# DeltaNet with an FNet block on one core: another way to the inverses of the first three rounds, a rebuilt first chain and earlier loads

## The chip, the cores and the metric

The kernel runs on one core of a Trainium2 chip. The metric is the device time in microseconds (us). Engines are named as in the profile: PE (TensorE, matmuls), PEld (its weight loads), DVE (VectorE), ACT (ScalarE), POOL (GpSimd), SP (SyncE, which here only issues DMAs).

## The reference

Four sequences of 768 tokens, 8 heads of 48, go through a delta rule; the output, 384 wide, goes through an FNet block. All in float32 (the weights come as float64).

```python
for t in range(S):
    kt, vt, bt = (k_n[:, :, t], v[:, :, t], beta[:, :, t, None])
    y[:, :, t] = np.einsum('bhd,bhde->bhe', q[:, :, t], state)
    v_old = np.einsum('bhde,bhd->bhe', state, kt)
    state = state + bt[:, :, :, None] * np.einsum('bhd,bhe->bhde', kt, vt - v_old)
...
X = np.fft.fft(x, axis=1)
X = np.fft.fft(X, axis=2)
mixed = np.real(X).astype(np.float32)
u = x + mixed
...
ch = np.maximum(un @ w_ch1, 0.0) @ w_ch2
return (u + ch).astype(np.float32)
```

`k_n` is k divided by its norm, `un` is u with mean and variance taken out.

## The kernel before

A tile `g` is 128 tokens of all 8 heads of one batch; a batch has 6 tiles (`NL`), there are 24. A chunk (`c`) is 64 tokens (`C`); inside a chunk the recursion is solved by the inverse of a unit lower triangular 64 x 64 matrix for every head. Four tiles (`RL`) make a round `r`; its matrices are inverted together.

- `pre_a(g)` turns the keys of a tile (KT) and forms their Gram products: the diagonal 32 x 32 blocks go to `G`, the blocks beside them to `GX` (X).
- `invert(r)`: 1024 blocks of 32 x 32 lie as 128 partitions x 8 x 4 after a 32 x 32 transpose on DVE (line 312). Norms follow (319 to 343, the root on ACT), then forward substitution: 31 steps, each a product `tmp` (353) and a sum into `M` (357). Two transposes (360, 361) bring the result back, into `A` and `G`.
- `pre_m(g)` joins the two 32-blocks of a chunk: two batches of 16 products of 32 x 32 (G,GX and A,XM), whose results ACT copies to XM and MT (419, 430). V is scaled by the norms on POOL (402). For batch 0 it goes on to WT and U0, products of MT with K and V (445, 447).
- `pre_q(g)` turns queries (QT) and forms the masked products LQ with the keys; for batch 0 all six are made ahead, the mask on POOL (391).
- `step(g, c)` carries the state S over a chunk: a product with S, a subtraction on DVE (498 for batch 0, 476 later), a product with K, an addition on DVE (517). This is the chain from chunk to chunk. `outputs(g)` writes the tile of x (541, 551).
- `fourier(b)`: folds of x (568 to 579, the first two on POOL), sums over the sequence with the tables evt and odt (590), over the width with dtab (611), then norms (617 to 629). `mlp(b)` makes ph and hT (660, 662), po (668) and the output.
- `weights()` turns the float64 words into float32: 12 pieces, each a row of five steps over ACT, DVE and POOL (235 to 250), six of `w1` and six of `w2`; a piece waits for the buffers of the one before it.

Generators yield after a step of work, and the code at the end interleaves them. Batch 0 stands in a block where the order on PE, DVE, ACT and POOL is the order of the program (785): keys of rounds 0 and 1, `invert(0)` with `invert(1)` woven in, then a loop over 12 chunks (835) in which the chain, the next tile's `pre_m`, the rest of `invert(1)`, the conversion of `w1` and two of the three folds take turns; then keys of round 2 with the sums of `fourier(0)`. After it (865) the order is fixed on PE alone: `mlp(b)` is spread over the `period(g)` of the next batch (six slots each), and `invert(r + 1)` runs on DVE beside them; the first period with tiles of a new round drains it (763). At a batch's end `weave` (868) spreads 12 pieces of the mlp over `fourier(b)`.

Keys for `pre_a` are loaded into three rotating buffers `Cs`, queries into two (`Qs`), both by SP; a load waits until its buffer was turned.

Of the kernel before, what the change touches and what calls it, by code (L numbers as in the profile page):

```python
# [17 lines left out]
C = 64  # L18
L = 128
W = 32  # L20
RL = 4
RING = 7


def _consts(S, DM):
# [6 lines left out]
    pack = np.concatenate([ident, su, blk], axis=1)  # L32
# [27 lines left out]
def kernel(  # L60
# [79 lines left out]

    def load_c(g, engine=None):
        if g < NLT:
            (engine or nc.sync).dma_start(out=Cs[g % 3][:, :, 0:D], in_=rows(k, g))

    def load_q(g):
        if g < NLT:
            nc.sync.dma_start(out=Qs[g % 2][:, :, 0:D], in_=rows(q, g))
# [12 lines left out]
    def load_beta(r):  # L160
# [5 lines left out]
        while i < RL:  # L166
            b, n = divmod(RL * r + i, NL)
            m = min(RL - i, NL - n)
            for q4 in range(4):
                hh, blk = divmod(q4, 2)  # L170
                p0 = q4 * W + i * 8
                src = beta[b, 4 * hh:4 * hh + 4, n * L:(n + m) * L].rearrange(
                    "j (c b t) -> b c j t", b=2, t=W)[blk]
                nc.sync.dma_start(out=t[p0:p0 + 8 * m], in_=src)
            i += m
        betas[r] = t

    pack = const.tile([128, 128 + C + 2], F32, name="pack")
    nc.scalar.dma_start(out=pack, in_=cn["pack"].ap())
    load_c(0)  # L180
    load_c(1, nc.scalar)
    load_c(2)
    load_beta(0)
    ident = pack[:, 0:128]
    m_su = pack[:, 128:128 + C]
    m_blk = pack[:, 128 + C:128 + C + 2]

# [4 lines left out]
    w2 = const.tile([128, KF, DM], F32, name="w2")  # L192

    low_e = const.tile([128, 1], F32, name="low_e")
    nc.gpsimd.memset(low_e, -896.0)
    half_n = const.tile([128, GT], F32, name="half_n")
# [78 lines left out]
    def pre_a(g):  # L275

        K = Cs[g % 3]
        r, li = divmod(g, RL)
        KT = KTs[g] = wk.tile([128, 2, 2, 128], F32, tag="KT", bufs=RING, name="KT")
        turn(KT, K)  # L280
        load_c(g + 3)
# [3 lines left out]
        X = GXs[g] = wk.tile([128, 8, W], F32, tag="GX", bufs=8, name="GX")  # L285
        pg = ps_pair()
        for i in range(4):
            c, jj = divmod(i, 2)
            for q4 in range(4):
                for jp in range(2):  # L290
# [3 lines left out]
                    if blk:  # L294
# [4 lines left out]
        nc.scalar.activation(Gs[r][:, 8 * li:8 * li + 8].rearrange("p (i a) s -> p a i s", a=2),  # L299
                             src[:, :, :, 0:W], ACT.Copy)  # L300
        nc.scalar.activation(X.rearrange("p (i a) s -> p a i s", a=2), src[:, :, :, W:C],
                             ACT.Copy)
        yield

    def invert(r):
# [3 lines left out]
        M = wk.tile([128, W, W], F32, tag="x" if r == 1 else "M", bufs=2 if r == 1 else 1,  # L309
                    name="M")  # L310
# [53 lines left out]

    LQs = {}

    def pre_q(g, QT=None, LQ=None):

        Q, KT = Qs[g % 2], KTs[g]
        early = QT is not None  # L370
# [5 lines left out]
        load_q(g + 2)  # L376
# [12 lines left out]
        if early:  # L389
            nc.scalar.activation(dst, src, ACT.Copy)  # L390
            nc.gpsimd.tensor_tensor(dst, dst, mask, op=ALU.mult)
        else:
            nc.vector.tensor_tensor(dst, src, mask, op=ALU.mult)
        yield

    def pre_m(g):

        r, li = divmod(g, RL)
        K, V, X = Ks[g % 3], Vs.pop(g), GXs.pop(g)
# [16 lines left out]
        XM = wk.tile([128, 8, W], F32, tag="XM", name="XM")  # L416
# [11 lines left out]
        for hh in range(2):  # L428
            rw = slice(64 * hh, 64 * hh + W)
            nc.scalar.activation(MT[rw, :, 1, :],  # L430
                                 py[rw, 0:8 * W].rearrange("p (m s) -> p m s", s=W), ACT.Copy)
        if g >= NL:
            pre[g] = (K, *LQs.pop(g), MT, V)
# [19 lines left out]
        pre[g] = (K, *LQs.pop(g), WT, U0)  # L453
        yield

    def step(g, c):
# [4 lines left out]
        if b > 0:  # L461
# [3 lines left out]
            K, QT, LQ, MT, V = pre[g]  # L465
# [22 lines left out]
        else:  # L488
            K, QT, LQ, WT, U0 = pre[g]
            U = U0[:, c]  # L490
# [29 lines left out]
    def outputs(g):  # L520

        b, n = divmod(g, NL)
        _, QT, LQ, _, U0 = pre.pop(g)
        if b > 0:
            U0 = Us[g]
# [32 lines left out]
    def fourier(b):  # L558
# [6 lines left out]
        O3 = wk.tile([128, 2, TH, DM], F32, tag="O", name="O3")  # L565
        O, EO, OO = O3[:, :, :, 0:MH], O3[:, :, :, MH:MH + ND], O3[:, :, :, MH + ND:DM]
        for t in range(TH):
            nc.gpsimd.tensor_tensor(E[:, 0, t], x[:, t], x[:, TH + t], op=ALU.add)
            nc.gpsimd.tensor_tensor(E[:, 1, t], x[:, t], x[:, TH + t], op=ALU.subtract)
            e, o = E[:, :, t], O[:, :, t]  # L570
            back = e[:, :, DM - 1:MH:-1]
            nc.vector.tensor_tensor(o[:, :, 1:MH], e[:, :, 1:MH], back, op=ALU.subtract)
            nc.vector.tensor_tensor(e[:, :, 1:MH], e[:, :, 1:MH], back, op=ALU.add)
            back = e[:, :, MH:ND:-1]
            nc.vector.tensor_tensor(EO[:, :, t], e[:, :, 0:ND], back, op=ALU.subtract)
            nc.vector.tensor_tensor(e[:, :, 0:ND], e[:, :, 0:ND], back, op=ALU.add)  # L576
            back = o[:, :, MH - 1:ND:-1]
            nc.vector.tensor_tensor(OO[:, :, t, 1:ND], o[:, :, 1:ND], back, op=ALU.subtract)  # L578
            nc.vector.tensor_tensor(o[:, :, 1:ND], o[:, :, 1:ND], back, op=ALU.add)
            yield  # L580

        F = wk.tile([ND + 1, 4, SEQ], F32, tag="F", name="F")
        parts = ((E, 0, ND + 1), (EO, 0, ND), (O, 1, ND + 1), (OO, 1, ND))
        for a in range(2):
            for par, tab, n, hi in ((0, evt, NE, HALF + 1), (1, odt, NO, HALF)):
                pa = ps_one()[:, 0:2 * n].rearrange("p (i k) -> p i k", i=2)
                for i in range(2):
                    src, d0, d1 = parts[2 * a + i]
                    for t in range(TH):
                        mm(pa[0:d1 - d0, i, :], src[:, par, t, d0:d1],  # L590
                           tab[:, t, a * n:a * n + n], i == 0 and t == 0, t == TH - 1)
# [9 lines left out]
        norms = []  # L601
# [30 lines left out]

        normed[b] = norms
# [90 lines left out]
    def period(g, side):  # L724
# [23 lines left out]
        if more:  # L748
            nq, pm = pre_q(g + 1), pre_m(g + 1)
            behind[0].append(nq)  # L750
            pieces[2].append(nq)
            pieces[3 if fresh else 1].append(pm)
# [159 lines left out]
```

## Time and profile before

| what | value |
|---|---|
| median of 3 runs | 808.28 us (807.11 to 810.37) |
| profiled execution | 811.8 us, span 809.9 us |
| mean granted clock of PE | 0.871 |
| PE busy | 686.8 us (85%) |
| PEld busy | 526.0 us (65%) |
| DVE busy | 391.5 us (48%) |
| ACT busy | 225.6 us (28%) |
| POOL busy | 132.4 us (16%) |
| chain that ended last | PE po 14%, PE ph 13%, PE one 4%, PE pair 3%; DVE M 2%, tmp 1% |

The page gives busy times over the whole span; the stages differ, so a row means little until it is asked for stage by stage. Times in the prediction count from the span's start. A row of the timeline has start, duration, engine, line, operation, output<-input and, in brackets, the idle time before it with what ended it. A float32 matmul shows as two records, so "x32" are 16 matmuls.

### The profile page before, as it was taken

The numbers are of one execution on the slowest core, as the hardware profiler recorded it, in microseconds if no ns is written. First come the engines' busy times: TensorE is split into PE (matmuls) and PEld (weight loads), VectorE is DVE, ScalarE is ACT, GpSimd is POOL, SyncE is SP. The second block draws the span as 40 slices with busy tenths as digits, with TensorE's granted clock in tenths as the row PEclk, the third lists the DMA queues.
The fourth block names the chain that finished last, engine by engine and source line by source line (L and its number), as shares of the span: only waits on it lengthen the run. The fifth ranks groups of instructions, "written<-read, shape, count | busy, mean of one in ns | idle before, by whom it ended". The sixth has DMA issues, their size and how long they took to land. (4 is left out here: it accounts for less than half of the span.)

```text
span 809.9 us, 22139 instructions
## 1 busy us (share of the span) xinstructions
PE 686.8 (85%) x9768; PEld 526.0 (65%) x9768; DVE 391.5 (48%) x932; ACT 225.6 (28%) x542; POOL 132.4 (16%) x150
## 2 busy tenths in 40 slices
PE   5536565388654998999998999989999999999998
PEld 4426565277542685677775776867767677786774
DVE  1898766548794239733438611998121141410000
ACT  4312333153410342122441223312323212221110
POOL 6132135403221000320001101211000020000000
PEclk8555555587765999999998999999999999999999
DMA  9821244312310331200221221101111000000000
GB/s 134 209 47 22 36 104 111 97 31 79 105 30 6 67 56 27 50 17 11 47 51 36 45 40 42 28 0 30 32 40 32 11 21 2 11 10 20 11 10 20
DMA packets 107378, 36.00 MB, mean 44 GB/s; under 512 B 99633, under 2 KB 102930, under 8 KB 107282
## 3 DMA queue, kind: packets, MB, share of 16 engines
q1 hardware_dynamic: 105586, 33.50, 18.8%
q8 instruction: 77, 1.26, 0.7%
q0 software_dynamic: 512, 0.79, 0.6%
q10 hardware_dynamic: 1184, 0.30, 0.2%
q14 instruction: 19, 0.16, 0.1%
HBM read 29.84 MB, written 4.72 MB: 43 GB/s over the span
## 5 line engine op out<-in xcount | busy, mean ns | idle before, releaser
L105 PE MATMUL po<-w,hT 128*128 128x384 f32 x576 | 210.6, 507 | 1.3 <-ACT unT L650 1.3
L105 PE MATMUL ph<-unT,w 128*128 128x256 f32 x864 | 202.4, 386 | 1.0 <-ACT unT L650 0.6
L105 PEld LDWEIGHTS ph<-unT,w 128*128 128x128 f32 x864 | 160.3, 191 | 25.3 <-ACT hT L662 1.2
L105 PEld LDWEIGHTS po<-w,hT 128*128 128x128 f32 x576 | 107.1, 195 | 61.1 <-issue 4.5
L662 ACT ACTIVATE hT<-ph 128x256 f32<-128x256 f32 x144 | 54.9, 383 | 156.6 <-PE ph L105 156.5
L672 DVE TENSOR_TENSOR x<-x,po 128x384 f32<-128x384 f32 x24 | 13.2, 551 | 146.7 <-PE po L105 146.7
L357 DVE TENSOR_TENSOR M<-M,tmp 128x135 f32<-128x135 f32 (+15 forms) x186 | 72.6, 392 | 5.3
L353 DVE TENSOR_TENSOR tmp<-A,M 128x60 f32<-128x60 f32 (+15 forms) x186 | 71.6, 387 | 4.7
L406 POOL TENSOR_TENSOR MT<-A,pack 128x512 f32<-128x512 f32 x24 | 26.5, 1107 | 244.8 <-PE one L105 174.3
L517 DVE TENSOR_TENSOR S<-S,pair 128x192 f32<-128x192 f32 x40 | 13.8, 345 | 89.4 <-PE pair L105 89.4
L105 PEld LDWEIGHTS one<-V,MT 64*64 64x64 f32 x768 | 36.6, 161 | 18.2 <-issue 9.3
L105 PE MATMUL one<-V,MT 64*64 64x48 f32 x768 | 42.3, 247 | 3.5 <-DVE V L476 2.7
L105 PE MATMUL one<-G,GX 32*32 32x32 f32 x768 | 19.5, 207 | 24.6 <-DVE G L361 24.6
L105 PEld LDWEIGHTS pair<-U,K 64*64 64x64 f32 x704 | 17.0, 156 | 28.0 <-DVE U L498 13.2
L105 PEld LDWEIGHTS one<-dtab,F 97*128 97x128 f32 (+1 forms) x192 | 27.8, 214 | 10.4 <-issue 3.0
L105 PE MATMUL pair<-U,K 64*64 64x48 f32 x704 | 22.9, 251 | 13.1 <-DVE U L498 12.1
L430 ACT ACTIVATE MT<-one 32x256 f32<-32x256 f32 x48 | 17.9, 373 | 57.7 <-PE one L105 55.5
L105 PEld LDWEIGHTS one<-G,GX 32*32 32x32 f32 x768 | 16.7, 121 | 26.2 <-DVE G L361 15.1
L476 DVE TENSOR_TENSOR V<-V,pair 128x192 f32<-128x192 f32 x33 | 11.6, 352 | 45.1 <-PE pair L105 38.3
L419 ACT ACTIVATE XM<-one 32x256 f32<-32x256 f32 x48 | 18.0, 375 | 52.6 <-PE one L105 52.2
L402 POOL TENSOR_TENSOR V<-V,nT 128x384 f32<-128x384 f32 x24 | 20.5, 854 | 73.1 <-DMA V<-in_v_dram 48.5
L105 PE MATMUL one<-dtab,F 97*128 97x97 f32 (+1 forms) x192 | 28.6, 299 | 4.5 <-DVE x L618 4.5
(114 smaller groups left out, 889.0 us busy)
## 6 DMA issues: line engine op xcount, KB each, us to landing
w<-in_moe_w_ch_dram SPq DMA_DIRECT2D x12, 768.0 KB
Q<-in_q_dram SPq DMA_DIRECT2D x24, 192.0 KB
out_dram<-x SPq DMA_DIRECT2D x24, 192.0 KB
C<-in_k_dram SPq DMA_DIRECT2D x23, 192.0 KB
K<-in_k_dram SPq DMA_DIRECT2D x88, 48.0 KB
V<-in_v_dram SPq DMA_DIRECT2D x88, 48.0 KB
evt<-k_even SPq DMA_DIRECT2D x1, 579.0 KB
odt<-k_odd SPq DMA_DIRECT2D x1, 576.0 KB
```

The source lines that it names most:

```text
L105: nc.tensor.matmul(o, lhsT=lhsT, rhs=rhs, start=start, stop=stop, skip_group_check=True)
L353: nc.vector.tensor_tensor(t, A[:, j + 1:W, j:j + 1].broadcast_to([128, n, j + 1]), M[:, j:j + 1, 0:j + 1].broadcast_to([128, n, j + 1]), o ...
L357: nc.vector.tensor_tensor(M[:, j + 1:W, 0:j + 1], M[:, j + 1:W, 0:j + 1], t, op=ALU.add)
L402: nc.gpsimd.tensor_tensor(V.rearrange("p c j d -> p (c j) d"), V.rearrange("p c j d -> p (c j) d"), nT[:, m8, None].broadcast_to([128, 8, ...
L406: nc.gpsimd.tensor_tensor(MT, MTd[:, m8, None, :].broadcast_to([128, 8, 2, W]), m_blk[:, None, :, None].broadcast_to([128, 8, 2, W]), op=A ...
L419: nc.scalar.activation(XM[rw].rearrange("p m s -> p (m s)"), px[rw, 0:8 * W], ACT.Copy, scale=-1.0)
L430: nc.scalar.activation(MT[rw, :, 1, :], py[rw, 0:8 * W].rearrange("p (m s) -> p m s", s=W), ACT.Copy)
L476: nc.vector.tensor_tensor(R4, R4, pw[:, :, 0:2 * D].rearrange("p a (j e) -> p a j e", e=D), op=ALU.subtract)
L517: nc.vector.tensor_tensor(s1v, s0.rearrange("p h j e -> p h (j e)"), pk, op=ALU.add)
L662: nc.scalar.activation(hT[:, fc, :], ph, ACT.Relu)
L672: nc.vector.tensor_tensor(x[:, T, :], x[:, T, :], po, op=ALU.add)
```

## The change

- Keys 0 to 7 and the six queries of batch 0 get places of their own, nine of them in the space that w2 will take; they are loaded without waiting. Loads of beta go to POOL's queue, and the table of the root is loaded at the start.
- Rounds 0 to 2 (`R16 = 3`): `gram16` forms whole 64 x 64 Gram products; `GU` keeps those between different blocks of 16 tokens. `invert16` substitutes inside blocks of 16 (15 steps instead of 31, two blocks side by side). `pre_m16` joins the four blocks of a chunk with a product series: ND is the negative product of GU with the inverse blocks, and three times MT is added to ND times the last result; the addition is itself a product, of MT with the identity, into the same accumulator. All are over whole 64 x 64 chunks. `V` is scaled on DVE for tiles 0 to 7.
- The first chain: two tiles are made before the loop, each turn of the loop works on `pre_m16(g + 2)`, the last part of g + 1 and the chain of g. Eight matmuls on an empty operand (`spin`) stand before it. DVE's other work is given out in small portions by `fill`; what is left of the w1 conversion comes after the loop.
- `fourier` is cut in two. `folds(b)` is on DVE for batch 0; for batches 1 to 3 it comes before the weave, whose slots go from 13 to 10.

```diff
+    def home(g):
+        return Cs[g] if g < 3 else Qs[g - 3] if g < 5 else early[g - 5] if g < 8 else Cs[g % 3]
...
+    early = w2.rearrange("p c m -> p (c m)").rearrange("p (n h d) -> p n h d", h=8, d=64)
+    nc.vector.memset(early[:, :, :, D:64], 0.0)
+    early = [early[:, i] for i in range(9)]
+    load_c(0)
...
-    load_c(0)
     load_c(1, nc.scalar)
-    load_c(2)
-    load_beta(0)
+    load_beta(0, nc.gpsimd)
+    for i in range(2, 2 * RL):
+        load_c(i)
...
-        K = Cs[g % 3]
         r, li = divmod(g, RL)
         KT = KTs[g] = wk.tile([128, 2, 2, 128], F32, tag="KT", bufs=RING, name="KT")
-        turn(KT, K)
-        load_c(g + 3)
+        turn(KT, home(g))
+        if g >= 2 * RL:
+            load_c(g + 3)
...
+        G = Gs[r][:, 8 * li:8 * li + 8]
+        if r < R16:
+            gram16(g, KT, G)
+            yield
+            return
...
+    def gram16(g, KT, G):
...
+        if first:
+            GU = GXs["O"][:, g]
+        else:
+            GU = wk.tile([128, 8, C], F32, tag="GX", bufs=4, name="GU")
+            nc.gpsimd.memset(GU[:, :, 0:V16], 0.0)
+        GXs[g, 16] = GU
+        pg = ps_pair()
+        for i in range(4):
+            c, jj = divmod(i, 2)
+            for hh in range(2):
+                for jp in range(2):
+                    kt = KT[lo[jp], hh, jj, c * C:c * C + C]
+                    mm(pg[full[hh], jp, C * i:C * i + C], kt, kt, i == 0)
+        src = pg[:, :, 0:4 * C].rearrange("p a (i s) -> p a i s", s=C)
+        dst = G.rearrange("p (i a) s -> p a i s", a=2)
+        nc.scalar.activation(dst, src[:, :, :, 0:W], ACT.Copy)
+        for hh in range(2):
+            rw = slice(64 * hh + W, 64 * hh + C)
+            if first:
+                nc.vector.tensor_copy(dst[rw], src[rw, :, :, W:C])
+            else:
+                nc.scalar.activation(dst[rw], src[rw, :, :, W:C], ACT.Copy)
+        dst = GU.rearrange("p (i a) s -> p a i s", a=2)
+        if first:
+            nc.vector.tensor_tensor(dst, src, m_up[:, None, None, :].broadcast_to([128, 2, 4, C]),
+                                    op=ALU.mult)
+        else:
+            for e in range(1, 4):
+                cs = slice(V16 * e, V16 * e + V16)
+                nc.scalar.activation(dst[:, :, :, cs], src[:, :, :, cs], ACT.Copy,
+                                     scale=m_ahead[:, e - 1:e])
...
+    def invert16(r):
...
+        nc.vector.scalar_tensor_tensor(bn, n2, -1.0, betas.pop(r), op0=ALU.mult, op1=ALU.mult)
+        yield
+        nc.vector.tensor_tensor(Ad, Ad, pairs(bn)[:, :, :, None].broadcast_to([128, 2, V16, V16]),
+                                op=ALU.mult)
+        nc.vector.tensor_scalar(ddiag, bn, -1.0, None, op0=ALU.mult)
...
+        for j in range(V16 - 1):
+            n = V16 - 1 - j
+            t = wk.tile([128, 256], F32, tag="tmp", bufs=2, name="tmp")
+            t = t[:, 0:2 * n * (j + 1)].rearrange("p (e a b) -> p e a b", e=2, a=n)
+            sh = [128, 2, n, j + 1]
+            nc.vector.tensor_tensor(t, Ad[:, :, j + 1:V16, j:j + 1].broadcast_to(sh),
+                                    Md[:, :, j:j + 1, 0:j + 1].broadcast_to(sh), op=ALU.mult)
+            yield
+            nc.vector.tensor_tensor(Md[:, :, j + 1:V16, 0:j + 1], Md[:, :, j + 1:V16, 0:j + 1], t,
+                                    op=ALU.add)
+            yield
+        nc.vector.transpose(G.rearrange("p m s -> p s m"), M.rearrange("p t s -> p s t"))
+        yield
+        nc.vector.transpose(A.rearrange("p m t -> p t m"), M)
+        rounds[r] = (A, G, nT)
+        yield
...
-        if early:
-            nc.scalar.activation(dst, src, ACT.Copy)
-            nc.gpsimd.tensor_tensor(dst, dst, mask, op=ALU.mult)
-        else:
-            nc.vector.tensor_tensor(dst, src, mask, op=ALU.mult)
+        nc.vector.tensor_tensor(dst, src, mask, op=ALU.mult)
...
+    def pre_m16(g):
...
+        m8 = slice(8 * li, 8 * li + 8)
+        tags = ("QT", "LQ") if g < 2 * RL else ("WT", "WT")
+        Z = wk.tile([128, 8, 2, W], F32, tag=tags[0], bufs=2, name="Z")
+        for e in range(2):
+            nc.scalar.activation(Z[:, :, e, :], Md[:, m8, :], ACT.Copy, scale=m_blk[:, e:e + 1])
+        px = ps_one()
+        for m in range(8):
+            for hh in range(2):
+                mm(px[full[hh], C * m:C * m + C], GU[full[hh], m, :],
+                   Z[full[hh], m].rearrange("p b t -> p (b t)"), m == 0)
+        ND2 = wk.tile([128, 8, C], F32, tag=tags[1], bufs=2, name="ND")
+        nc.scalar.activation(ND2.rearrange("p m t -> p (m t)"), px, ACT.Copy, scale=-1.0)
+        MT = wk.tile([128, 8, 2, W], F32, tag="MT", bufs=2, name="MT")
+        for e in range(2):
+            nc.scalar.activation(MT[:, :, e, :], MTd[:, m8, :], ACT.Copy, scale=m_blk[:, e:e + 1])
+        flat = "p m b t -> p (m b t)"
+        yield
+        for i in range(3):
+            pz = ps_one()
+            mm(pz, ident, MT.rearrange(flat), True, False)
+            src = Z if i else MT
+            for m in range(8):
+                for hh in range(2):
+                    mm(pz[full[hh], C * m:C * m + C], ND2[full[hh], m, :],
+                       src[full[hh], m].rearrange("p b t -> p (b t)"), False)
+            nc.scalar.activation((MT if i == 2 else Z).rearrange(flat), pz, ACT.Copy)
+            if i < 2:
+                yield
+        V = Vs.pop(g)
+        (nc.vector if g < 2 * RL else nc.gpsimd).tensor_tensor(
+            V.rearrange("p c j d -> p (c j) d"), V.rearrange("p c j d -> p (c j) d"),
+            nT[:, m8, None].broadcast_to([128, 8, D]), op=ALU.mult)
         if g >= NL:
-            pre[g] = (K, *LQs.pop(g), MT, V)
...
         for t in range(TH):
-            nc.gpsimd.tensor_tensor(E[:, 0, t], x[:, t], x[:, TH + t], op=ALU.add)
-            nc.gpsimd.tensor_tensor(E[:, 1, t], x[:, t], x[:, TH + t], op=ALU.subtract)
+            eng = nc.gpsimd if b else nc.vector
+            eng.tensor_tensor(E[:, 0, t], x[:, t], x[:, TH + t], op=ALU.add)
+            yield
+            eng.tensor_tensor(E[:, 1, t], x[:, t], x[:, TH + t], op=ALU.subtract)
...
+        def sums(a, par, tab, n, ts):
+            if ts[0] == 0:
+                pas[a, par] = ps_one()[:, 0:2 * n].rearrange("p (i k) -> p i k", i=2) if b else \
+                    ps_post([128, 2, n], "pf")
+            pa = pas[a, par]
+            for i in range(2):
+                src, d0, d1 = parts[2 * a + i]
+                for t in ts:
+                    mm(pa[0:d1 - d0, i, :], src[:, par, t, d0:d1], tab[:, t, a * n:a * n + n],
+                       i == 0 and t == 0, t == TH - 1)
...
+            for par, tab, n, hi in tabs:
+                if b or a:
+                    sums(a, par, tab, n, range(TH))
+                elif par == 0:
+                    for p2, t2, n2, _ in tabs:
+                        sums(0, p2, t2, n2, range(TH - 1))
+                    yield
+                    for p2, t2, n2, _ in tabs:
+                        sums(0, p2, t2, n2, (TH - 1,))
...
-            nq, pm = pre_q(g + 1), pre_m(g + 1)
+            nq = pre_q(g + 1)
             behind[0].append(nq)
             pieces[2].append(nq)
-            pieces[3 if fresh else 1].append(pm)
-            pieces[5 if fresh else 3].append(pm)
+            if g + 1 >= RL * R16:
+                pm = pre_m(g + 1)
+                pieces[3 if fresh else 1].append(pm)
+                pieces[5 if fresh else 3].append(pm)
+            elif g + 1 >= 2 * RL:
+                pm = pre_m16(g + 1)
+                for i in range(4):
+                    pieces[i + (2 if fresh else 0)].append(pm)
...
-            if i == 3 and fresh and inv:
+            if i == (2 if r + 1 < R16 else 3) and fresh and inv:
...
+        nc.gpsimd.memset(idle, 0.0)
+        def spin(n):
+            for _ in range(n):
+                nc.tensor.matmul(unread[:, 0:DM], lhsT=ident, rhs=idle, start=True, stop=True,
+                                 skip_group_check=True)
...
         for g in range(RL):
-            if g + 1 < RL:
-                advance(keys[g + 1])
-            drain(keys[g])
-        load_q(0)
-        load_q(1)
-        for g in range(2):
-            load_k(g, nc.gpsimd)
-            load_v(g, nc.gpsimd)
-        load_beta(1)
+            advance(keys[g])
+            if g > 0:
+                drain(keys[g - 1])
+        drain(keys[RL - 1])
+        advance(inv0, 2)
+        for g in range(3):
+            load_q(g)
+        load_k(0)
+        load_v(0)
+        load_beta(1, nc.gpsimd)
+        load_q(3)
+        load_k(1, nc.gpsimd)
...
+        for g in range(RL, 2 * RL - 1):
+            advance(keys[g])
+            if g > RL:
+                drain(keys[g - 1])
+        drain(keys[-2])
+        advance(qs[0])
+        drain(inv0)
         drain(qs[0])
-        advance(keys[7])
-        drain(keys[6])
-        drain(keys[7])
-        advance(inv0, 20)
-        advance(inv1, 2)
-        nc.sync.dma_start(out=evt, in_=cn["even"].ap())
-        nc.sync.dma_start(out=odt, in_=cn["odd"].ap())
...
+        drain(keys[-1])
+        advance(qs[1])
+        spin(8)
+        advance(ms[0])
+        advance(inv1)
+        spin(1)
+        advance(ms[0])
+        advance(inv1)
+        advance(ms[1])
...
+        advance(inv1, 3)
+        advance(ms[1])
+        conv = side
+        first = part(side, 30)
+        fd = None
+        def fill(n):
+            while n > 0 and advance(inv1):
+                n -= 1
+            while n > 0 and fd and advance(fd):
+                n -= 1
+            advance(first, n - 1)
+        for g in range(NL):
+            c0, c1 = step(g, 0), step(g, 1)
+            nm, n2 = ms[g + 1], ms[g + 2]
+            load_k(g + 2)
+            load_v(g + 2)
+            if g > 0:
+                advance(c0)
+                fill(3)
+                drain(late)
...
+                if g == 4:
+                    fold = folds(0)
+                if g >= 4:
+                    fd = part(fold, 8)
+            advance(n2)
+            advance(c0)
+            fill(3)
+            if g + 1 < NL:
+                drain(nm)
+            advance(n2)
+            advance(c1)
+            fill(3)
+            if g + 1 < NL:
+                drain(qs[g + 1])
+            advance(n2)
+            if g + 1 < NL:
+                advance(c1)
+                fill(3)
+                if g + 2 < NL:
+                    advance(qs[g + 2])
+                advance(n2)
+            else:
+                drain(n2)
+            late = outputs(g)
+            if g == 1:
...
+        drain(late)
+        late = None
+        load_beta(2)
+        drain(first)
+        drain(fd)
+        drain(fold)
         f = fourier(0)
...
         keys = [pre_a(g) for g in range(2 * RL, 3 * RL)]
         advance(f)
         for k4 in keys:
             advance(k4)
             advance(f)
             advance(k4)
+        advance(conv)
         drain(f)
-        inv = invert(2)
+        inv = invert16(2)
     with tc.manual_schedule(engines={mybir.EngineType.PE}):
         for b in range(B):
             if b > 0:
-                weave([(fourier(b), 1)], side, KEEP, 13)
+                drain(folds(b))
+                weave([(fourier(b), 1)], side, KEEP, 10)
```

## The prediction

> **What bounds the kernel now.** I read the page's slices first, then busy time by stage, then the waits of TensorE, then the timeline around those waits.
>
> ```profile
> span 809.9 us, 22139 instructions
> PE   5536565388654998999998999989999999999998
> DVE  1898766548794239733438611998121141410000
> PEclk8555555587765999999998999999999999999999
> ```
>
> One slice is 20.2 us. From slice 13 on TensorE (PE) is full; before it PE is half idle, mostly at half clock, and VectorE (DVE) is full. My stages (us, then busy us of PE, weight loads, DVE, ScalarE, GpSimd, clock, DMA share, GB/s):
>
> ```profile
> 16.30:69.80 53.50, 26.84 (x619) 21.09 (x617) 47.84 (x117) 16.35 (x34) 13.79 (x12) 0.50 0.44 102
> 69.80:153.90 84.10, 49.99 (x1367) 45.92 (x1368) 58.83 (x112) 26.30 (x49) 26.66 (x21) 0.52 0.30 69
> 153.90:177.30 23.40, 16.41 (x330) 14.01 (x329) 6.22 (x11) 9.06 (x25) 3.75 (x3) 0.85 0.36 100
> 177.30:253.40 76.10, 47.96 (x548) 39.01 (x548) 66.58 (x158) 22.74 (x46) 17.64 (x15) 0.68 0.21 57
> 253.40:300.00 46.60, 45.97 (x859) 33.61 (x860) 8.26 (x14) 15.98 (x40) 4.68 (x5) 0.93 0.28 53
> 300.00:560.00 260.00, 246.92 (x3513) 184.99 (x3512) 155.85 (x401) 72.81 (x190) 35.11 (x40) 0.98 0.16 32
> ```
>
> These are: first inverse to first state product; the loop over batch 0; folds and sequence sums; a DVE window that ends with the third round's inverse; then PE. The timeline shows both ends of DVE chains on which PE waits:
>
> ```profile
> 62.18 1.06 PE L105 MATMUL one<-G,GX 32*32 32x32 f32 x32 [9.55 <-DVE G L361]
> 253.39 1.06 PE L105 MATMUL one<-G,GX 32*32 32x32 f32 x32 [15.00 <-DVE G L361]
> ```
>
> So before 253.4 a DVE microsecond is worth something, after it only a PE microsecond is. The change trades DVE for PE on both sides of that line. Prices:
>
> ```profile
> 24.14 0.25 DVE L353 TENSOR_TENSOR tmp<-A,M 128x87 f32<-128x87 f32 x1
> 25.33 0.30 DVE L353 TENSOR_TENSOR tmp<-A,M 128x135 f32<-128x135 f32 x1
> 463.88 0.67 PE L105 MATMUL one<-V,MT 64*64 64x48 f32 x16
> 464.48 2.86 PE L105 MATMUL ph<-unT,w 128*128 128x256 f32 x12
> 509.42 0.69 PE L105 MATMUL one<-G,GX 32*32 32x32 f32 x32
> 516.61 0.69 PE L105 MATMUL one<-A,XM 32*32 32x32 f32 x32
> ```
>
> A float32 matmul is two records. The V,MT batch starts 0.60 us before the next batch: 16 records in 0.60.
>
> **The Trainium skill.** "TensorE: Matmul & The Clock Gate", section What's actually happening: the array runs at half clock until it was busy for about 3.4 us, and falls back after an idle window of that length. The trace agrees: 16 records pair<-S,WT take 0.56 us at 92.1, after about 5 us of unbroken work, and 0.68 at 96.4, after 2.6 us of idleness. The same page, section The mechanism: a weight load overlaps a running matmul only in another row group. The trace agrees: V,MT has two chains (each half of the rows), so eight records a chain take 75 ns each, of which streaming 48 columns at the rate of ph (0.215 us for 256) is 40; some 35 ns of the load is left bare. "GPSIMD Engine Reference", section 8. Key points: GpSimd shares SBUF interfaces with VectorE and is about half as fast elementwise. Agrees: the mask of LQ takes 1.44 us on POOL and 0.69 on DVE, and the DVE update beside it at 26.35 took 1.26 instead of 0.32.
>
> **The change, step by step.**
>
> *Round 0's inverse.* 62 updates become 30 with 30 to 128 elements. From the rows above these are 0.20 to 0.30 us, mean 0.26, plus 0.035 between: 8.8 us. Eight key tiles load at once into free space, so the last Gram tile should be there at about 14; its DVE copies and mask (0.38+0.38+0.69) bring the first transpose to 15.5. Then 1.9 (transpose), 0.6 (root on ACT, table loaded ahead), 3.1 (eleven small operations), 1.1 (scaling), 8.8, 1.9 (transpose back): ready at 33, against 62. The masks of the early LQ leave POOL, so nothing collides. Queues: SP issues the C tiles at about 0.55 us each with no buffer to wait for, so Q0 to Q2, K0 and V0 go out by 10 us; behind them come Q3 to Q5 and the weights, needed 15 us later or more. Beta moves to POOL's queue, behind 2 us of memsets, and is needed at 21. The scaling of V moves to DVE (about 0.55 each, ahead of the next subtraction of the chain, which has 1 us in hand).
>
> *The idle products.* ACT has about 2.6 us for each of key tiles 4 to 7 and two query copies; PE reaches the eight filler matmuls near 31.6. They are like po (0.70 us each at full clock, 1.4 at half): 7 to 8 us. Z would be ready at 34, so they cost 0 to 5; I take 3: start at 37, with a warm clock.
>
> *A product series (pre_m16).* Sixteen products with 64 moving columns in two chains: 16 records a chain at 53+30 ns = 1.35 us. The identity product streams 512 columns: 0.9. A tile has px and three times (identity + products): 1.35 + 3 x 2.25 = 8.1 us, where the old tile had two batches of 0.62: +6.85. This is the largest unknown, as the trace has no such batch. Its floor is streaming alone, 16 x 53 = 0.85 a batch, 6.1 a tile; its ceiling is the half clock, 15. I take 8.1, because V,MT shows bare loads.
>
> *First chain.* Two tiles before the loop, interleaved: ND, MT and Z copies (0.6 to 0.8 each on ACT) leave small gaps; adding them in order gives 21 us: loop at 58, against 69.8. A turn of the loop on PE: outputs 1.15, wait for Z 0.85, series 8.1, WT and U0 1.85, steps 1.2, query tile 1.25: 14.4. Round 0 lacks outputs, the last lacks WT and the query: 12.5 + 4 x 14.4 + 11 = 81, +2 where the weight conversion blocks DVE. Loop end 141, last output 142.5: the loop takes 83 us, as long as before (84.1), because what DVE no longer does PE does.
>
> *Tail.* The fills give the conversion 2 of its steps each: of 30 steps 18 are done in the loop, 12 remain. Its chain from ACT to DVE to POOL and back (0.9, 0.96, 0.56, 0.94, 0.56, 0.96, 1.85, with hops 7 us a piece; consecutive pieces wait for each other's buffers) takes 15.6 us with nothing beside it; then ten fold operations, 5.8. Folds end at 164.5, where they ended at 160.4. The C tiles, tables and folds on DVE instead of POOL change little: DMA and POOL are idle there. Sums and keys: ACT has 3.2 us a key tile now; 16.5 us, so norms start at 181 (177.3 before).
>
> *DVE window.* Of its 66.6 us busy, 16.5 go with the smaller substitution (62 x 0.39 to 30 x 0.26), 2 with the order of the transposes, 0.6 with scaling; some POOL collisions too. 76 becomes 55: PE gets the third round's inverse at 236, against 253.4: 17 earlier.
>
> *After it.* PE is 95 to 99% busy, so four tiles (8 to 11) at +6.85 cost 27.4. Off that: 3.5 of idle time near 310 to 330 that gets filled, 2.5 for the cold stretch 254 to 260. On top: 1.4 for one pair of po products that is not yet done, and about 4 (0 to 9) at the batch ends, where the folds of batches 1 to 3 now stand before all filler pieces (three pieces, 3.9 us, covered each until now). Net +26.8.
>
> Sum: 236 + 556.5 + 26.8 = 819.3 against the span of 809.9: +9.4. The profiled execution lay at 811.8, 3.5 over the median of 808.28; on the median that is **818 us**.
>
> **Rivals.**
> 1. *Loads hidden.* If weight loads are pulled ahead in these longer batches, a tile costs 6.1: 2.0 less for about seven tiles before 236 and for four after: 22, so 796. For it: the four-chain batches need only 18 ns a record (QT,KT, 0.58 for 32). Against it: two-chain V,MT. It decides from a tile price of 6.5 us down. This is the case on the other side.
> 2. *The window shrinks further.* If the conversion's tail overlaps with keys, or the inverse is placed in the waits of the conversion, 236 becomes 226: 808, no change. Against it: the conversion's chain alone is 43 us in the window.
> 3. *Cold loop.* If gaps in the loop reach the 2.6 us that dropped the clock at 96, half the loop at half clock adds 35: 853. Against it: no PE gap in my order exceeds 1.5 us.
>
> **How the numbers follow.** Forecast 0.50 (its own range 806 to 832), rival 1 0.26, rival 2 0.16, rival 3 0.08. The range: down to 790 (rival 1 with nothing lost at the batch ends), up to 842 (start of the loop, tail and batch ends each 6 to 9 worse); outside lie about 0.07 above and 0.08 below. About 0.5% is what a measurement of this kernel can tell from no change. Faster by more: 0.24 from rival 1, 0.05 from rival 2: 0.29. Within: 0.12. Slower: 0.59.
>
> **What would show it.** Right, if the round-0 inverse ends at 33 +- 3; if 16 products with 64 columns take about 1.35 us from start to start at full clock; if a turn of the loop takes 14 to 15; if POOL and DVE work on the conversion with PE idle for 15 us after the loop; if the first product of tile 8 starts near 236 and PE is full from there to the end. Wrong, if the series costs 6 a tile, if PE fills the tail, or if PE has gaps after 236 in which the added products hide.

## The result and the profile after

The changed kernel takes **842.4 us** (median of 4 runs, 839.69 to 844.61) against 809.33 beside it: ratio 1.041, 95% interval 1.037 to 1.046. The direction was forecast, the size was not: +33 us where +9.4 was put, just outside the range.

The page of the profile after, its slices (21.1 us each now):

```profile
span 842.8 us, 23085 instructions
PE   5888876636959999899998999969999999999998
DVE  5723544446992119641618811798221123320000
PEclk9999989757959999999999999989999999999999
```

VectorE is no longer full at the start and TensorE is no longer cold there, as meant. But TensorE still only becomes full from the thirteenth slice on, at 253 us. The same five stages by their busy time (columns as in the prediction: length, PE, weight loads, DVE, ScalarE, GpSimd, clock, DMA share, GB/s):

```profile
39.30:63.70 24.40, 20.57 (x398) 13.91 (x398) 5.77 (x23) 9.38 (x20) 0.00 (x0) 0.93 0.22 37
63.70:160.70 97.00, 77.50 (x1972) 59.36 (x1967) 44.44 (x99) 39.41 (x74) 6.40 (x4) 0.88 0.21 50
160.70:199.40 38.70, 16.61 (x205) 14.10 (x203) 17.87 (x26) 17.99 (x46) 6.03 (x7) 0.74 0.29 83
199.40:253.70 54.30, 39.84 (x400) 33.65 (x400) 52.71 (x122) 20.40 (x40) 15.43 (x13) 0.72 0.29 79
253.70:842.80 589.10, 563.69 (x6938) 415.37 (x6938) 214.29 (x541) 154.26 (x390) 55.21 (x66) 0.98 0.12 27
```

First chain, loop over batch 0, tail with folds and sums, DVE window, and the rest. Set beside the forecast: first S to last x add take 97.0, where 84.5 was put (58 to 142.5); tail and sums 38.7, where 38.5 was put (142.5 to 181); the window 54.3 for 55. Tile 8's first product starts at 253.67, where the kernel before had it at 253.39. So the 17 us that were to be won on that line were not won at all, and behind it TensorE needs 589.1 instead of 556.5.

The timeline of TensorE in the loop shows where its 97 us go. These are the first products of tiles 4, 5, 6 and 7, one a turn, and tile 7's next step:

```profile
94.42 1.83 PE L110 MATMUL one<-Z,GU 64*64 64x64 f32 x29 [3.65 <-ACT Z L578]
112.07 1.83 PE L110 MATMUL one<-Z,GU 64*64 64x64 f32 x29 [3.01 <-ACT Z L578]
131.04 1.46 PE L110 MATMUL one<-Z,GU 64*64 64x64 f32 x29 [4.28 <-ACT Z L578]
147.17 1.05 PE L110 MATMUL one<-Z,GU 64*64 64x64 f32 x29 [3.01 <-ACT Z L578]
149.80 2.07 PE L110 MATMUL one<-MT,pack 128*128 128x512 f32 x2 [1.26 <-ACT MT L588]
```

Each of these turns begins with a wait of 3.0 to 4.3 us for Z, and after most of them the clock is down: 1.83 instead of 1.05 for the same batch, 2.07 instead of 1.13 for an identity product. What ScalarE and VectorE did in the gap of tile 7, before 147.17:

```profile
143.34 0.95 DVE L260 SCALAR_TENSOR_TENSOR man<-num,man 128x768 f32<-128x768 int32 x1
144.33 0.56 DVE L263 TENSOR_SCALAR num<-w 128x768 int32<-128x768 int32 x1
144.93 0.93 ACT L265 ACTIVATE num<-num,low_e 128x768 int32<-128x768 int32 x1 [1.58 <-DVE num L263]
145.77 0.47 ACT L715 ACTIVATE x<-pair 128x384 f32<-128x384 f32 x1
146.14 0.89 ACT L578 ACTIVATE Z<-G,pack 128x256 f32<-128x256 f32 x2
```

L265 and L263 belong to the weight conversion. ScalarE keeps the order of the program here: the Z copies stand behind a conversion step that waits for VectorE, and behind the last tile's x copy. Z's own input was there long before; the second inverse was back in G at 93.3. The gap of tile 4, before 94.42, is another case. There Z waits for that inverse (ScalarE's waits from 63.7 to 160.7):

```profile
ACT Z L578 <- DVE G L495: 2.8, 1, 2.8
```

In the tail and at the batch ends (waits of TensorE, from 160 to 253 and from 253 on: total, times, longest):

```profile
PE pf L110 <- DVE E L757: 18.0, 1, 18.0
...
PE one L110 <- DVE E L757: 10.2, 3, 6.6
```

The first is the conversion's tail ahead of the folds, as forecast. In the kernel before, the second was, from 253.4 us on:

```profile
PE one L105 <- DVE E L576: 2.9, 1, 2.9
```

### The profile page after: what moved, and what is told of

It is laid out like the page before. It is cut to its first block, busy times and chain, and to the rows that moved or that the text cites. A ratio compares the mean times of both kernels' runs of the same rounds, so it can differ in the third digit from the quotient of the medians.

```text
span 842.8 us, 23085 instructions
## 1 busy us (share of the span) xinstructions
PE 745.3 (88%) x10242; PEld 556.1 (66%) x10242; DVE 361.4 (43%) x869; ACT 258.8 (31%) x612; POOL 99.2 (12%) x132
## 5 line engine op out<-in xcount | busy, mean ns | idle before, releaser
L110 PE MATMUL one<-MT,pack 128*128 128x512 f32 x72 | 44.1, 697 | 1.9 <-ACT MT L588 1.9
L110 PEld LDWEIGHTS one<-Z,ND 64*64 64x64 f32 x768 | 25.0, 138 | 20.0 <-issue 17.7
L422 DVE TENSOR_TENSOR M<-M,tmp 128x31 f32<-128x31 f32 (+15 forms) x93 | 35.0, 376 | 2.9
L110 PE MATMUL one<-Z,GU 64*64 64x64 f32 x384 | 17.6, 257 | 19.9 <-ACT Z L578 19.9
L418 DVE TENSOR_TENSOR tmp<-A,M 128x31 f32<-128x31 f32 (+15 forms) x93 | 33.1, 356 | 2.8
L539 POOL TENSOR_TENSOR MT<-A,pack 128x512 f32<-128x512 f32 x12 | 12.7, 1057 | 163.3 <-PE one L110 139.3
L599 ACT ACTIVATE Z<-one 128x512 f32<-128x512 f32 x24 | 14.3, 597 | 53.2 <-PE one L110 53.2
L110 PEld LDWEIGHTS one<-Z,GU 64*64 64x64 f32 x384 | 15.9, 167 | 21.4 <-issue 14.9
L110 PE MATMUL pair<-KT 48*32 48x64 f32 (+1 forms) x1152 | 22.8, 248 | 6.9 <-ACT KT L295 6.6
L110 PE MATMUL one<-Z,ND 64*64 64x64 f32 x768 | 28.4, 225 | 0.0
```

The lines of the kernel that those rows point to most:

```text
L110: nc.tensor.matmul(o, lhsT=lhsT, rhs=rhs, start=start, stop=stop, skip_group_check=True)
L418: nc.vector.tensor_tensor(t, A[:, j + 1:W, j:j + 1].broadcast_to([128, n, j + 1]), M[:, j:j + 1, 0:j + 1].broadcast_to([128, n, j + 1]), o ...
L422: nc.vector.tensor_tensor(M[:, j + 1:W, 0:j + 1], M[:, j + 1:W, 0:j + 1], t, op=ALU.add)
L539: nc.gpsimd.tensor_tensor(MT, MTd[:, m8, None, :].broadcast_to([128, 8, 2, W]), m_blk[:, None, :, None].broadcast_to([128, 8, 2, W]), op=A ...
L599: nc.scalar.activation((MT if i == 2 else Z).rearrange(flat), pz, ACT.Copy)
```

## The experiments

All are edits of the changed kernel, each timed beside the kernel before.

**1. The third round back to the 32-token substitution** (tiles 8 to 11 by `pre_m`).

```
-R16 = 3
+R16 = 2
...
-        inv = invert16(2)
+        inv = invert(2)
```

> The product series stays for the first two rounds; the third round (tiles 8 to 11) goes back to the 32-token substitution and its two short batches. Theory (the series is paid on TensorE, about 6.2 us a tile): 4 tiles give back 25 us after the third inverse, and the inverse itself takes 17 to 20 us longer on VectorE, so 843 becomes 835 to 838. Rival (after the third inverse the added products lie in waits that were there anyway): nothing is given back, the longer inverse stays, 860. Rival (the longer substitution hides in the window behind the norms and the conversion): 818 to 822.

Measured 836.66 us, ratio 1.033 (1.030 to 1.036). By busy time, from the third inverse to the end:

```profile
272.60:836.90 564.30, 537.69 (x6638) 399.45 (x6638) 211.91 (x538) 145.72 (x376) 58.93 (x69) 0.98 0.13 28
```

The inverse comes at 272.6, 19.9 later than its 252.7, and 564.3 us follow instead of 590.1 (842.8 - 252.7): 25.8 less, 6.45 a tile. The first theory holds. The products were not hidden, and VectorE's saving of 19.9 us was real; it was worth less than the products cost.

**2. The folds of batches 1 to 3 woven between MLP pieces again.**

```
-                drain(folds(b))
-                weave([(fourier(b), 1)], side, KEEP, 10)
+                fb, yb = folds(b), fourier(b)
+                def both():
+                    while advance(fb, 8):
+                        yield
+                    yield from yb
+                weave([(both(), 1)], side, KEEP, 13)
```

> Only the folds of batches 1 to 3 are woven between pieces of the MLP again, as in the kernel before. Theory (TensorE waits 10 us at three batch ends for E, where it waited 2.9): 843 becomes 835 to 837. Rival (the pieces that cover the folds are then missing in the sums and key tiles behind them, so the wait only moves): 842 to 843.

Measured 835.12 us, ratio 1.032 (1.030 to 1.035): 7.3 less. Its waits of TensorE, after 250 us:

```profile
PE one L110 <- DVE E L757: 2.8, 1, 2.8
```

10.2 became 2.8, and the difference of 7.4 is the gain: the wait didn't move on.

**3. The next tile's first series stage ahead of the conversion steps and the late outputs.** The stage is `advance(n2)`; `fill(3)` issues conversion steps and `drain(late)` the outputs; what is left of the second inverse (`inv1`) stays ahead of the stage.

```
                 advance(c0)
+                if g == 2:
+                    drain(inv1)
+                advance(n2)
                 fill(3)
                 drain(late)
-                if g == 2:
-                    drain(inv1)
...
-            advance(n2)
+            else:
+                advance(n2)
```

> In the loop over batch 0 the next tile's first series stage goes out ahead of the conversion steps and of the late outputs, so that its Z copies stand first in ScalarE's queue. Theory (the Z waits of 16 us between 60 and 165, and the half clock after them, make the loop 14 us longer than I put it): the loop ends 8 to 12 us earlier and 843 becomes 831 to 835. Rival (the wait moves to ND and the x copies, since ScalarE itself waits for VectorE in the conversion): 840 to 843.

Measured 836.4 us, ratio 1.033 (1.030 to 1.037): 6.0 less, half of what I had put; the loop takes 92.5. Tiles 5 to 7 now begin so:

```profile
109.39 1.05 PE L110 MATMUL one<-Z,GU 64*64 64x64 f32 x29 [1.85 <-issue]
...
125.88 1.83 PE L110 MATMUL one<-Z,GU 64*64 64x64 f32 x29 [3.10 <-issue]
...
141.63 1.05 PE L110 MATMUL one<-Z,GU 64*64 64x64 f32 x29 [1.32 <-issue]
```

The gaps shrink from 3.01, 4.28 and 3.01 to 1.85, 3.10 and 1.32; the profile no longer names a releaser. The gap of tile 4 doesn't (4.13). The edit puts Z ahead of two things at once, a conversion step and the x copy, and their shares in these 4.5 us of the loop were not separated. One place in the order was moved; conversion steps of the other places in a turn are still ahead of the later stages.

**4. What is left of the conversion behind the folds**, three steps to a key tile.

```
-        drain(first)
         drain(fd)
         drain(fold)
...
             advance(f)
+            advance(first, 3)
             advance(k4)
+        drain(first)
         advance(conv)
```

> What is left of the first part of the weight conversion after the loop no longer stands ahead of the folds; it is spread over the four key tiles behind the sums. Theory (TensorE is empty for 18 us only because the folds queue behind the conversion): norms start 10 to 13 us earlier, third inverse too, 843 becomes 830 to 833. Rival (ScalarE bounds the key tiles, and the conversion steps on it add their full time there): norms start only 2 to 4 us earlier, 839 to 841.

Measured 830.65 us, ratio 1.026 (1.022 to 1.029): 11.8 less, the largest single part. The last part of the first sums, on the timeline:

```profile
164.65 0.57 PE L110 MATMUL pf<-evt,E 128*97 128x193 f32 x2 [1.10 <-DVE E L757]
```

The wait of 18.0 is 1.10, and the norms start at 186.98 instead of 199.44, although the conversion's steps are done in the same stretch. They fit beside the key tiles.

**5. No conversion step in the loop at all**, with edits 3 and 4; six steps to a key tile, the rest after.

```
-            advance(first, n - 1)
...
+            advance(first, 6)
```

> The Z copies ahead and the conversion behind the folds, as in the two runs before, and no conversion step in the loop over batch 0 at all: its 30 steps stand behind the folds, six to a key tile and the rest after them. Theory (conversion steps in ScalarE's queue are what keeps Z late, and the half clock follows from these waits): the loop, from the first S to the last x add, takes 82 to 86 us instead of 97, close to the 83 of my prediction; the conversion then costs about the same again in front of the norms or the third inverse, so 820 to 830. Rival (the series itself with its dependence product, copy, product makes the loop long): the loop stays at 91 to 93 and the total rises to 836 or more.

Measured 846.56 us. The loop is what this run is for: its row by busy time, and the first products of tiles 4 to 7.

```profile
63.60:150.00 86.40, 72.68 (x1972) 54.91 (x1967) 32.94 (x81) 32.40 (x66) 0.98 (x1) 0.94 0.15 28
```

```profile
91.88 1.83 PE L110 MATMUL one<-Z,GU 64*64 64x64 f32 x29 [4.15 <-issue]
...
109.42 1.05 PE L110 MATMUL one<-Z,GU 64*64 64x64 f32 x29 [1.31 <-issue]
...
124.13 1.05 PE L110 MATMUL one<-Z,GU 64*64 64x64 f32 x29 [1.31 <-issue]
...
138.23 1.05 PE L110 MATMUL one<-Z,GU 64*64 64x64 f32 x29 [1.31 <-issue]
```

The loop takes 86.4 instead of 97.0, with TensorE busy 72.7 instead of 77.5 at a clock of 0.94 instead of 0.88. The last two starts lie 14.7 and 14.1 behind the ones before them: the 14.4 of my turn. So the order on ScalarE and VectorE costs TensorE 10.6 of the 12.5 us that the loop was too long: 4.5 came with edit 3, the other 6.1 with the last conversion steps. The work of a turn was priced about right in sum. One gap of 4.15 us stays, at tile 4, whose Z waits for the second inverse's transpose into G (88.84 to 90.84); with the half clock behind it that turn takes 17.5. The total missed its expectation: with 30 steps behind the folds the norms start at 208.76, TensorE waits 20.4 us for KT in all, and the third inverse is back only at 250.4. The conversion has to run somewhere, and this place is the dearer one.

**6. Without the nine filler products.**

```
-        spin(8)
...
-        spin(1)
```

> The nine filler products ahead of the first series are taken out, nothing else. Theory (they hold TensorE 4 to 5 us beyond the readiness of Z, and buy a warm clock): the first product of tile 0 starts near 35 instead of 39, but the first chain then runs at half clock and the first S comes no earlier than 1 to 3 us; 841 to 843. Rival (they are pure delay): first S 4 to 5 us earlier, 837 to 838. Rival (they are needed): the first chain takes more than 5 us longer, 845 or more.

Measured 843.77 us, ratio 1.043 (1.039 to 1.047) against 1.041: no difference that these runs could tell. Tile 0's first product and identity product, on the timeline:

```profile
34.66 1.97 PE L110 MATMUL one<-Z,GU 64*64 64x64 f32 x32 [2.44 <-ACT Z L578]
38.12 2.08 PE L110 MATMUL one<-MT,pack 128*128 128x512 f32 x2 [1.49 <-ACT MT L588]
```

It starts at 34.66 instead of 39.34, at half clock (1.97 and 2.08 instead of 1.15 and 1.13), and the first S is there at 62.63, inside what the runs with filler have (60.9 to 63.7). Delay and warmth cancel, as far as this spread can tell.

**7 and 8. Edits 2, 3 and 4 together; then edit 1 as well.**

> Folds woven, Z copies ahead, conversion behind the folds, all three together; the product series in all three rounds as in the changed kernel. Theory (the three losses are separate: 7, 6 and 12 us): 817 to 819. Rival (the last two share one cause, ScalarE waiting for VectorE in the conversion): 822 to 825.

> The same three edits, and the 32-token substitution in the third round. Theory (separate costs, another 6 us): 811 to 813. Rival (with the conversion behind the folds VectorE has more in the window, and the longer inverse is paid in full there): 817 to 820. A result under 807 would need the window to hide part of the inverse.

Measured 817.08 us (ratio 1.011, 1.006 to 1.015) and 810.65 us (1.003, 1.001 to 1.004). The single gains sum to 7.3 + 6.0 + 11.8 = 25.1, with edit 1 (5.7) to 30.8, which from 842.4 gives 817.3 and 811.6. Within the spread of these runs (814.2 to 820.8 in the first) the costs are separate and add up.

**9. The series in the first round alone**, on top of 2, 3 and 4. Rounds two and three have the 32-token substitution; tiles 4 to 7 go through `pre_m`, which for batch 0 goes on to WT and U0 as `pre_m16` does.

```
-R16 = 3
+R16 = 1
...
-            if g + 1 >= RL * R16:
+            if g + 1 >= RL * max(R16, 2):
...
-        inv0, inv1 = invert16(0), invert16(1)
+        inv0, inv1 = invert16(0), invert(1)
...
-        ms = [pre_m16(g) for g in range(2 * RL)]
+        ms = [pre_m16(g) if g < RL else pre_m(g) for g in range(2 * RL)]
...
-        advance(inv1, 3)
+        advance(inv1, 7)
...
-        inv = invert16(2)
+        inv = invert(2)
```

> The three edits stay; only the first round (tiles 0 to 3) keeps the 16-token substitution and the series, rounds two and three have the 32-token substitution. Theory (in the loop TensorE is on the path and each series costs it 6.2 us, while VectorE has room there): four tiles give back up to 25 us of the loop, VectorE gets 18 more in the loop and the conversion steps that no longer fit there, so the third inverse comes 6 to 20 us earlier than with two rounds of series: 791 to 805, under the kernel before. Rival (VectorE sets the third inverse over the whole stretch): 811 plus up to 18, 815 to 829.

Measured **798.1 us**, ratio 0.986 (0.983 to 0.989). Loop, tail with window, and the rest, by busy time:

```profile
59.80:143.30 83.50, 61.80 (x1692) 52.46 (x1684) 52.16 (x105) 30.34 (x58) 17.06 (x13) 0.67 0.28 67
143.30:241.90 98.60, 63.39 (x753) 52.07 (x751) 81.58 (x181) 31.95 (x68) 21.20 (x16) 0.71 0.25 68
241.90:798.20 556.30, 536.89 (x6638) 399.29 (x6638) 211.21 (x538) 145.23 (x376) 58.27 (x69) 0.98 0.13 28
```

The last row is that of the kernel before to 0.2 us (556.50, 537.05, x6638). So the whole gain is that the third inverse comes at 241.9 instead of 253.4, 11.5 earlier, and 10.0 of that is there when the loop starts: at 59.8 instead of 69.8. The loop itself takes what it took before (83.5 for 84.1).

**10 and 11. In the loop every conversion step behind a series stage**: edit 3 at all three places, on top of run 8 and of run 9.

```
             advance(c0)
-            fill(3)
             if g + 1 < NL:
                 drain(nm)
             advance(n2)
+            fill(3)
             advance(c1)
```

> Three edits and series in two rounds, and in the loop all conversion steps go out behind the next series stage, not only at the first of the three places. Theory (each remaining Z copy still waits about 1 us behind a conversion step on ScalarE): the loop is 3 to 5 us shorter than its 92, total 806 to 808. Rival (the steps then delay the S and U updates on VectorE by as much): 810 to 812.

> Both of these together. Theory: with fewer series in the loop there are fewer Z copies to be late, so 1 to 3 us better than the first round alone, 790 to 803. Rival: no difference between the two, or the updates on VectorE come later, up to 3 us worse.

Measured 817.77 us and 803.87 us: 7.1 and 5.8 more than without it (5.5 and 5.4 by the ratios to the kernel before). Both theories fell, and both rivals were too mild. ScalarE and VectorE around 104 us of run 10:

```profile
104.07 0.60 ACT L599 ACTIVATE Z<-one 128x512 f32<-128x512 f32 x1 [3.04 <-PE one L110]
104.56 0.93 ACT L265 ACTIVATE num<-num,low_e 128x768 int32<-128x768 int32 x1
105.52 0.56 DVE L267 TENSOR_SCALAR num<-num 128x768 int32<-128x768 int32 x1 [7.63 <-ACT num L265]
105.99 0.35 DVE L673 TENSOR_TENSOR U<-U,pair 128x192 f32<-128x192 f32 x1
```

Now the conversion's ScalarE step stands behind a Z copy that waits for TensorE; VectorE stands 7.63 us waiting for that step, and the U update of the state chain behind it. The wait was passed to the other queue, and the loop takes 98.8 us (run 8: 92.6).

**12. In the first two turns five steps of the second inverse at a place, instead of three**, on top of 9.

```
-                fill(3)
+                fill(5 if g < 2 else 3)
```

> The kernel with series in the first round alone, and in the first two turns of the loop five steps of the second inverse where three stood, so that fewer are left in one block ahead of tile 4. Theory (TensorE waits 7.4 us for that block while VectorE had idle gaps before it): the second inverse ends 3 to 5 us earlier, the loop with it, 794 to 796. Rival (VectorE is already full there, and the steps only stand ahead of the S updates): 797 to 800.

Measured **793.63 us**, ratio 0.981 (0.978 to 0.984), the fastest of all. TensorE's wait for the second inverse, in run 9 and then in this one:

```profile
PE one L110 <- DVE G L426: 7.4, 1, 7.4
```

```profile
PE one L110 <- DVE G L426: 1.8, 1, 1.8
```

The second inverse's transpose ends 6.2 us earlier (85.1 for 91.3), the loop only 3.4 (139.9 for 143.3): TensorE's waits for the x copies grow from 4.6 to 12.4 us. In these two executions the stretch from the loop to the third inverse is 3.7 shorter as well; why is open.

## Why the prediction was wrong

The step that failed is the turn of the loop: "wait for Z 0.85" and "+2 where the weight conversion blocks DVE". The other work of the turn was right in sum (run 5). The waits for Z were 0.9, 3.65, 3.0, 4.3 and 3.0 us, some 15 where five times 0.85 stood. I had priced Z by its own copies and not by what stands ahead of them on ScalarE: conversion steps that wait for VectorE, and the last tile's x copy. The last three waits are 1.3 each in run 5. I charged the conversion to VectorE, when it reaches TensorE through ScalarE. The wait of 3.65 at tile 4 is another omission: Z waits there for the second inverse, for which the turn had no term, and no edit of the place of Z took that away (4.1 to 4.2 in runs 3, 5 and 7). The half clock behind these gaps adds some 5 (TensorE busy 77.5 against 72.7 in run 5). Together this is more than the 12.5 us that were missing; the cheaper series (below) took some back. Rival 3, at 0.08, named the clock but not the queue, and its size was wrong, 35 us for the 5 here. It was set low because "no PE gap in my order exceeds 1.5 us", the same error.

In the order of the sum:
- Round 0's inverse at 33: its transpose into G ends at 33.2. Right. The first product was put at 37 and starts at 39.34, the first chain at 21 and takes 24.3, so the loop starts at 63.7, 5.7 late. Up to 2.8 of this is the spread of single executions: with the same code up to there the first S comes between 60.9 and 63.7. The filler is not the cause (run 6); which of the small gaps in that chain is was not tried.
- Tile price 8.1, or +6.85: it is +6.45 (run 1). Right in sum by luck, through two errors that partly cancel. Behind 253.7 its two kinds of product stand side by side on the timeline:

```profile
258.24 1.13 PE L110 MATMUL one<-MT,pack 128*128 128x512 f32 x2
259.30 1.15 PE L110 MATMUL one<-MT,ND 64*64 64x64 f32 x32
260.38 2.85 PE L110 MATMUL po<-w,hT 128*128 128x384 f32 x8
```

From start to start the identity product takes 1.06, not 0.9, and the sixteen products 1.08, not 1.35 (the sum itself took 30 ns of bare load a record, where its own reading of V,MT gave 35; with 35 it would have been further off). Four batches and three identity products are 7.5, where 8.1 stood. Rival 1 (6.1 a tile, and decisive from 6.5 down) is wrong.
- Loop, 84.5 put: 97.0.
- Tail 15.6 and folds 5.8: 160.7 to 181.8, 21.1 for 21.4. Right in size (from 142.5 they end at 163.9; the 164.5 of the prediction is a slip of 0.6). I took it as given; run 4 shows that its order costs 12.
- Sums and keys 16.5: 17.6. DVE window 55: 54.3. Both right. So the third inverse was 17.7 late (253.7 for 236): 5.7 from the start of the loop and 12.5 from the loop, less half a microsecond.
- After it +26.8: +32.6. The tiles are 25.8 for 27.4, the batch ends 7.3 (run 2) for 4, inside their 0 to 9. The 6 us that were to come off (idle time that gets filled, a cold stretch that warms up) don't show in the total: at the batches' own prices four tiles are 4 x (7.5 - 1.24) = 25.0, and what they cost net is 25.8. In run 1, with the old tiles, the stretch is 564.3 against 556.5 before, and the folds account for nearly all of that.

Together 17.7 + 5.8 = 23.5, which is what separates the span of 842.8 from the sum's 819.3.

Why the kernel became slower follows from the same runs. Undoing the parts gives back 5.7 (series in the third round, net of the longer inverse), 7.3 (folds), 6.0 (conversion and outputs ahead of Z) and 11.8 (conversion ahead of the folds). With all four undone the loop starts 8.7 us earlier than in the kernel before and takes 8.5 longer (61.1 and 92.6 in run 8), and the times are level. With the series left to the first round the loop is as short as before and the earlier start is kept (runs 9 and 12). The early loads with the old inverse in all rounds were not tried, so their own share in that start, beside the shorter first inverse, stays open.

## What to carry to other kernels

Price a wait by the queue and not by the instruction: ask what stands ahead of it on its engine, and what that waits for. A helper chain that goes back and forth between two engines meets the main chain wherever the two queues cross; moving it by one place made that 6 us better, by another 7 us worse. A saving on one engine that another engine pays is worth it only as long as the first one sets the end. For tiles 4 to 7 (run 9 against run 8) and 8 to 11 (run 1) the series cost more than it saved. The fastest kernels kept it for the first four tiles; whether it pays even there was not tried, as no kernel had the early loads without it.

## What the runs showed of the hardware that was not expected

- Sixteen float32 products with 64 columns (16 records in each of two chains) take 1.08 us, eight with 48 columns (8 in each) 0.60. Per record of a chain that is 67 and 75 ns, the longer one for fewer columns. Less the streaming at the rate of ph (53 and 40 ns) that leaves 14 and 35 ns: the part of a weight load that lies bare is not a constant that can be added to the streaming time, as I had done. What sets it is open. The identity product takes 1.06 where streaming at the rate of ph (2 x 512 columns) gives 0.86.
- The length of the last gap doesn't tell the clock. After gaps of 1.3 us the batch ran at full clock (1.05, run 5). After gaps of 3.01 it took 1.83 at 112.07, but 1.05 at 147.17, where only what followed was slow (2.07 at 149.80). At tile 3 it took 1.87 after a gap of 0.91, with one of 1.95 shortly before:

```profile
75.11 0.49 PE L110 MATMUL pair<-S,QT 48*64 48x48 f32 x10 [1.95 <-DVE pair L705]
...
77.15 1.87 PE L110 MATMUL one<-Z,GU 64*64 64x64 f32 x30 [0.91 <-ACT Z L578]
```

  The Trainium skill, "TensorE: Matmul & The Clock Gate", section What's actually happening, has the activity window free-running; equal gaps with different outcomes agree with that. But it puts the idle window that drops the clock at about 3.4 us, and every gap named here is shorter, as was the one of 2.6 us that the prediction called an agreement. What share of idle time inside a window is enough isn't shown.
- Filler products that keep TensorE warm ahead of a chain with small gaps were worth about what they cost: 842.4 us with them, 843.8 without, and 1.4 us is within the spread of the runs.
